# Attention over chunks of 64 tokens and a squared-ReLU feed-forward: token groups formed inside batches, queries loaded token by token, and later slots for the attention steps

## Chip, cores and metric

The kernel runs on one core of a Trainium2 chip. The metric is the device time of the core in microseconds; smaller is better. Times are medians over several executions, and a profile is one execution.

## What is computed

Attention inside chunks of 64 tokens, for 8 batches, 8 heads, 576 tokens (nine chunks) a batch and 64 numbers a head; then a feed-forward layer with a squared ReLU over all 4608 tokens. Inputs and output are float32.

```python
q_c, k_c, v_c = (x.reshape(B, H, S // 64, 64, D) for x in (q, k, v))
scores = np.matmul(q_c, k_c.transpose(0, 1, 2, 4, 3)) / np.sqrt(D)
attn = softmax(scores)
x = np.matmul(attn, v_c)            # back to (B * S, H * D) = (4608, 512)
h = np.maximum(x @ w_in, 0.0)       # w_in 512 x 2048
out = h * h @ w_out                 # w_out 2048 x 512
```

## The kernel before

**Groups and blocks.** The 4608 tokens are cut into 18 groups of 256 (`GT`), in the order of the flat token number. As a batch has 576 tokens, many groups reach over a batch's end; `segments` cuts their loads there, so such a group has more and smaller loads. Two groups make a block of the feed-forward (`blocks`, line 41); there are nine blocks, and the second one takes its groups as [3, 2].

**Loads** all go through the SP queue, in program order. `qk_pieces(g)` loads q and k of a group, `v_pieces(g)` its values, the even heads into `ve_sb` tiles and the odd heads into `vo_sb` tiles; these lie 64 tokens askew, so that a matmul on half of the array finds its chunk in the right half of the partitions. In the types of the load: q comes as pairs of tokens (512 contiguous bytes), k of groups 0 to 3 too, k of the others and v token by token (256 bytes). Ten q and k buffers (five each), five `ve_sb` and eleven `vo_sb` buffers take turns.

**Attention of a group** in steps, named by letters in the schedule: C (`cast_qk`, line 213) makes bfloat16 of q and k, on GpSimd (POOL) for groups under 8, else on ScalarE (ACT); TD (`transpose_qk_dma`, line 223) transposes both with one DMA from the SP queue into `qkT`; SC (`scores`, line 231) does 32 small matmuls on TensorE (PE) and one exponential on ACT; AV (`values`, line 259) does 32 matmuls, and VectorE (DVE) divides by the sums into `x`; XT (`transpose_x`, line 287) transposes x, for groups from 6 on by a DMA from the SP queue. Groups 0 to 3 are transposed on PE instead (TA, TE, TQ, TK). In `scores`, the function `queries` picks the right side of the matmul: for groups from 4 on, the tokens of a pair lie apart in `qkT`, and it reads them with a stride.

**Feed-forward of a block.** `ffn_in` is 16 slots, in each of which PE does four matmuls of 512 columns (line 336), ACT the ReLU (347), DVE or ACT the square (351, 349). Block 1 does it in two halves of 256 columns, so 32 slots. `ffn_out` is 14 slots: a form of the product with seven half products instead of eight (line 404), whose sums DVE makes; results are stored from POOL's queue (`store`, line 420). Block 0 does a plain product (485).

**The order is written out by hand.** [...]In the loop at line 546, the block j gives each slot of its feed-forward at most one load of a later block (`go_slots`) and, by `plan`, the attention steps of the next block's groups (`nxt`: SC, AV, XT) and of the one after it (`far`: C, TD). From block 2 on, `loads` are those of `far`. So SP's queue holds, for each block: loads, two XT, two TD, and the rest; whatever stands behind a transpose waits for that transpose's input.

Of the kernel before, what the change touches and what calls it, by code (L numbers as in the profile page):

```python
# [11 lines left out]
BF16 = mybir.dt.bfloat16  # L12
# [5 lines left out]
def kernel(  # L18
# [22 lines left out]
    blocks = [[0, 1], [3, 2]] + [[g, g + 1] for g in range(4, n_grp, 2)]  # L41
# [34 lines left out]
    def segments(g0, n):  # L76
        while n:
            b, s = divmod(g0, S)
            m = min(n, S - s)
            yield b, s, m  # L80
            g0 += m
            n -= m

    qk = {}

    def runs(g):

        for t in range(GT // 128):
            p = 0
            for b, s, m in segments(g * GT + t * 128, 128):  # L90
                yield t, p, m, b, s
                p += m

    def qk_pieces(g):
# [3 lines left out]

        pairs = ((q_sb, q), (k_sb, k)) if g < FIRST_DMA_T else ((q_sb, q),)
        p = 0  # L100
        for b, s, m in segments(g * GT, GT):
            for dst, src in pairs:
                yield lambda dst=dst, src=src, b=b, s=s, p=p, m=m: nc.sync.dma_start(
                    out=dst.rearrange("p t h d -> p (t h d)")[p:p + m // 2, :].rearrange(
                        "p (h e) -> p h e", h=H),
                    in_=src[b, :, s:s + m, :].rearrange("h (s i) d -> s h (i d)", i=2))
            p += m // 2
        if g < FIRST_DMA_T:
            return
        for t, p, m, b, s in runs(g):  # L110
            yield lambda b=b, s=s, t=t, p=p, m=m: nc.sync.dma_start(
                out=k_sb[p:p + m, t, :, :],
                in_=k[b, :, s:s + m, :].rearrange("h s d -> s h d"))

    def v_pieces(g):

# [4 lines left out]
        for n in {0: [0, 1, 2], 2: [5], 3: [6, 7, 8]}.get(g, [2 * g + 1, 2 * g + 2]):  # L121
            lo, hi = max(0, 128 * n - 64), min(n_tokens, 128 * n + 64)
            p = lo - (128 * n - 64)
            for b, s, m in segments(lo, hi - lo):
                yield lambda n=n, p=p, m=m, b=b, s=s: nc.sync.dma_start(
                    out=v_odd[n % NO][p:p + m, :, 0:D],
                    in_=v[b, 1::2, s:s + m, :].rearrange("h s d -> s h d"))
                p += m
# [102 lines left out]
    def scores(g):  # L231
        qkT = state.pop(("qkT", g))

        def queries(a, t, hp, p):
            x = qkT[64 * a:64 * a + 64, 0]
            if g < FIRST_DMA_T:
                return x[:, t, hp, p * 64:p * 64 + 64]
# [397 lines left out]
```

## Time and profile before

| | us |
|---|---|
| median of 5 executions | 295.82 (290.96 to 297.7) |
| the profiled execution | 294.84 |
| its span, first to last instruction | 293.1 |
| PE busy in it | 275.6 |
| DVE busy | 190.7 |
| ACT busy | 161.9 |
| POOL busy | 53.5 |

The span is what the lines of a profile add up to; the time of an execution has 1.7 us more around it. Busy time is summed over an engine; a busy engine isn't necessarily the one that sets the end. In the answers of the trace, a line such as "153.96 0.69 PE L249 ..." reads: start in us, duration in us, engine, line of the kernel, what it writes and reads, and in brackets how long the engine had been idle and what ended that. SPq is SP's queue: its duration is the time to issue a DMA, the data arrives later.

The DMA queues in the page: 138,640 packets and 47.33 MB on SP's queue (q1), 2,832 packets and 9.18 MB on POOL's (q0). Typical times from issue to landing by its last part: k 256 KB 6.4 us, q 512 KB 6.8, v 128 KB 4.0, the transpose into qkT 5.6, that into xT 3.6.

### The profile page before, as it was taken

Reading aid. Unit: us, or ns where it says so; the run is one execution under the profiler, and the core shown is the slowest. Engines: PE = TensorE matmul, PEld = TensorE weight load, DVE = VectorE, ACT = ScalarE, POOL = GpSimd, SP = SyncE. Lnnn points to the kernel's source line nnn. Section 1 sums busy time; section 2 is a strip of 40 time slices with the busy share of each in tenths; the row PEclk is TensorE's granted clock in tenths of the full one; section 3 lists DMA queues with packets and bytes.
Section 4 is the critical chain, followed back from the end, with each engine's and each line's share of the span. In section 5 each row is a group of like instructions: output and inputs, shape, how many; then the busy total and the mean of one; then the engine's idle time right before and its main releaser. Section 6 shows DMA issues by size and latency. Waiting matters only on the chain.

```text
span 293.1 us, 7263 instructions
## 1 busy us (share of the span) xinstructions
PE 275.6 (94%) x3011; PEld 183.2 (63%) x3014; DVE 190.7 (65%) x305; ACT 161.9 (55%) x270; POOL 53.5 (18%) x85
## 2 busy tenths in 40 slices
PE   2999999999999999999959999999999999999994
PEld 1774444778774488448824686468547854784583
DVE  1157514899863495489634994698369738964793
ACT  1527605776348753866366656773777387317710
POOL 2037644042152003000200002001100210020012
PEclk9999999999999999999999999999999999999999
DMA  7999999997999999999999999998996841111003
GB/s 201 236 303 363 363 314 200 291 216 175 226 227 247 232 198 244 216 231 187 209 231 227 183 154 270 211 153 193 297 215 123 125 166 36 38 77 68 2 18 125
DMA packets 141648, 57.09 MB, mean 195 GB/s; under 512 B 110448, under 2 KB 137328, under 8 KB 141616
## 3 DMA queue, kind: packets, MB, share of 16 engines
q1 hardware_dynamic: 138640, 47.33, 75.6%
q0 software_dynamic: 2832, 9.18, 8.9%
q8 instruction: 23, 0.38, 0.6%
q10 hardware_dynamic: 144, 0.13, 0.1%
q14 instruction: 9, 0.07, 0.1%
HBM read 36.70 MB, written 9.44 MB: 157 GB/s over the span
## 4 chain that ended last, share of the span: by engine, by line
PE 82%; DMA 8%; DVE 5%; ACT 2%; issue 1%; SPq 0%; ACTq 0%
PE ps_ffn L336 36%; PE ps_ffn L404 32%; DMA qkT<-qkb 6%; PE ps_ffn L485 4%; PE ps_att L249 3%; PE ps_att L273 2%; DVE gT L351 2%; DMA k_sb<-in_k_dram 2%; PE ps_ffn L211 2%; DVE x L281 2%; ACT rl L347 1%; PE ps_ffn L165 1%; PE ps_att L300 1%; PE ps_ffn L200 0%; DVE w_out_bf L364 0%
## 5 line engine op out<-in xcount | busy, mean ns | idle before, releaser
L336 PE MATMUL ps_ffn<-xT,w_in_bf 128*128 128x512 bf16 (+1 forms) x640 | 130.5, 358 | 0.8 <-ACT rl L347 0.2
L351 DVE TENSOR_TENSOR gT<-rl 128x512 bf16<-128x512 f32 (+2 forms) x132 | 77.0, 607 | 65.1 <-ACT rl L347 63.5
L347 ACT ACTIVATE rl<-ps_ffn 128x512 f32<-128x512 f32 (+2 forms) x160 | 85.6, 553 | 34.7 <-PE ps_ffn L336 32.7
L336 PEld LDWEIGHTS <-w_in_bf 128*128 128x128 bf16 x640 | 60.6, 98 | 58.9 <-issue 1.5
L404 PEld LDWEIGHTS <-w_st 128*128 128x128 bf16 x640 | 62.3, 98 | 7.5
L423 POOL DMA_DIRECT2D out_dram<-o_sb x29 | 20.8, 717 | 159.4 <-DVE o_sb L364 153.9
L364 DVE TENSOR_TENSOR w_st<-gT 128x2048 bf16<-128x2048 bf16 x40 | 47.3, 1218 | 0.2
L404 PE MATMUL ps_ffn<-w_out_bf,w_st 128*128 128x256 bf16 x384 | 45.0, 273 | 0.0
L404 PE MATMUL ps_ffn<-w_sum,w_st 128*128 128x256 bf16 x256 | 29.6, 273 | 0.0
L404 PEld LDWEIGHTS <-gT 128*128 128x128 bf16 x256 | 25.0, 98 | 4.5
L281 DVE TENSOR_TENSOR x<-ps_att,rec 128x512 bf16<-128x512 f32 x36 | 24.9, 691 | 1.2
L475 ACT COPY o_sb<-ps_ffn 128x512 f32<-128x512 f32 (+1 forms) x8 | 4.5, 560 | 34.7 <-PE ps_ffn L404 34.7
L256 ACT ACTIVATE e<-ps_att 128x1024 bf16<-128x1024 f32 x18 | 17.9, 1020 | 10.0 <-PE ps_att L249 9.7
L349 ACT ACTIVATE gT<-rl 128x512 bf16<-128x512 f32 (+2 forms) x28 | 16.8, 599 | 0.9
L249 PE MATMUL ps_att<-qkT 64*64 64x64 bf16 x576 | 11.4, 219 | 4.3 <-DMA qkT<-qkb 4.0
L404 PE MATMUL ps_ffn<-w_out_bf,gT 128*128 128x256 bf16 x128 | 15.3, 273 | 0.0
L404 PE MATMUL ps_ffn<-w_sum,gT 128*128 128x256 bf16 x128 | 15.3, 272 | 0.0
L485 PE MATMUL ps_ffn<-w_out_bf,gT 128*128 128x512 bf16 x61 | 14.3, 379 | 0.6 <-ACT rl L347 0.3
L249 PEld LDWEIGHTS <-qkT 64*64 64x64 bf16 x576 | 8.8, 109 | 9.2 <-DMA qkT<-qkb 4.3
L273 PEld LDWEIGHTS <-e 64*64 64x64 bf16 x576 | 7.0, 107 | 9.1 <-DVE x L281 2.2
L140 POOL CAST w_in_bf<-w_st 128x1024 bf16<-128x1024 f32 (+1 forms) x9 | 8.6, 966 | 19.8 <-DMA w_st<-in_moe_w_in_dram 19.8
L273 PE MATMUL ps_att<-ve_sb,e 64*64 64x65 bf16 x288 | 9.9, 197 | 1.6 <-DVE x L281 0.7
(51 smaller groups left out, 164.7 us busy)
## 6 DMA issues: line engine op xcount, KB each, us to landing
out_dram<-o_sb POOLq DMA_DIRECT2D x33, 256.0 KB, 5.2
k_sb<-in_k_dram SPq DMA_DIRECT2D x25, 256.0 KB, 6.4
q_sb<-in_q_dram SPq DMA_DIRECT2D x12, 512.0 KB, 6.8
ve_sb<-in_v_dram SPq DMA_DIRECT2D x32, 128.0 KB, 4.0
vo_sb<-in_v_dram SPq DMA_DIRECT2D x32, 128.0 KB, 4.0
w_st<-in_moe_w_in_dram SPq DMA_DIRECT2D x8, 512.0 KB, 7.0
w_st<-in_moe_w_out_dram SPq DMA_DIRECT2D x8, 512.0 KB, 6.9
k_sb<-in_k_dram SPq DMA_DIRECT2D x3, 512.0 KB, 7.1
```

The source lines that it names most:

```text
L249: nc.tensor.matmul(out=ps[64 * c:64 * c + 64, o0:o0 + 64], lhsT=qkT[64 * a:64 * a + 64, 1, t, hp, cols], rhs=queries(a, t, hp, p), start=T ...
L256: nc.scalar.activation(out=e.rearrange("p a h t q -> p (a h t q)"), in_=ps, func=AF.Exp, scale=scale)
L273: nc.tensor.matmul(out=ps[64 * p:64 * p + 64, a, hp * (D + 1):(hp + 1) * (D + 1)], lhsT=e[64 * c:64 * c + 64, a, hp, t, :], rhs=vb[64 * c: ...
L281: nc.vector.tensor_tensor(out=x[:, t].rearrange("p h a d -> p a h d"), in0=o[:, :, :, 0:D], in1=rec.to_broadcast([128, 2, n_hp, D]), op=AL ...
L336: nc.tensor.matmul(out=h[:, 0:n], lhsT=w_in_bf[:, dt, ft * 128:(ft + 1) * 128], rhs=xT[:, c // 128:(c + n) // 128, dt, :], start=(dt == 0) ...
L347: nc.scalar.activation(out=rl[:, 0:n], in_=h[:, 0:n], func=AF.Relu)
L349: nc.scalar.activation(out=gT[:, ft, c:c + n], in_=rl[:, 0:n], func=AF.Square)
L351: nc.vector.tensor_tensor(out=gT[:, ft, c:c + n], in0=rl[:, 0:n], in1=rl[:, 0:n], op=ALU.mult)
L364: engine.tensor_tensor(out=out, in0=in0, in1=in1, op=op)
L404: nc.tensor.matmul(out=outs[t], lhsT=a[:, i, t * 128:(t + 1) * 128], rhs=b[:, i, :], start=(first and i == 0 and (last or t == 0)), stop=( ...
L423: dma.dma_start(out=out[t0:t0 + HT, col:col + HD].rearrange("(t p) d -> p t d", p=128), in_=o_sb.rearrange("p (t d) -> p t d", d=HD))
L485: nc.tensor.matmul(out=o_ps[tt], lhsT=gT[:, ft, tt * 128:(tt + 1) * 128], rhs=w_out_bf[:, ft, :], start=(ft == 0), stop=(ft == n_ft - 1))
```

## The change

1. Groups are formed inside batches: two groups of four whole chunks a batch, and the ninth chunk of each batch goes, four batches together, into two groups of their own, placed as groups 14 and 15 (block 7). Blocks are then simply pairs in order. `runs` gives the pieces of a group; a whole group has no cut.
2. q of groups from 4 on is loaded token by token in two loads, as k is; the cast and the scores read it in order (`queries` is gone). Groups 0 to 3 keep pairs.
3. The odd heads' tiles are laid out for two groups together: five tiles a pair of groups with loads of 64, 128, 128, 128 and 64 tokens (four loads of 128 before, cut at batch ends).
4. A ninth-chunk group is stored with two DMAs in place of one.
5. Slots: in block 1, one slot later for XT of the block's second group, and one earlier for SC, AV and XT of the next block's; in the others, SC, AV and XT mostly one slot later, with three slots between the two groups' AV.

```diff
-    blocks = [[0, 1], [3, 2]] + [[g, g + 1] for g in range(4, n_grp, 2)]
+    blocks = [[g, g + 1] for g in range(0, n_grp, 2)]
+    CH = GT // 4
+    n_ch = S // CH
+    whole = [[(b, CH * (4 * i + c)) for c in range(4)] for b in range(B) for i in range(2)]
+    rest = [[(b, CH * (n_ch - 1)) for b in range(b0, b0 + 4)] for b0 in range(0, B, 4)]
+    chunks = whole[:-2] + rest + whole[-2:]
+    def is_whole(g):
+        return chunks[g][0][0] == chunks[g][3][0]
...
     def runs(g):
-        for t in range(GT // 128):
-            p = 0
-            for b, s, m in segments(g * GT + t * 128, 128):
-                yield t, p, m, b, s
-                p += m
+        for t in range(2):
+            (b, s), (b1, s1) = chunks[g][2 * t:2 * t + 2]
+            if b == b1:
+                yield t, 0, 2 * CH, b, s
+            else:
+                yield t, 0, CH, b, s
+                yield t, CH, CH, b1, s1
...
         for t, p, m, b, s in runs(g):
-            yield lambda b=b, s=s, t=t, p=p, m=m: nc.sync.dma_start(
-                out=k_sb[p:p + m, t, :, :],
-                in_=k[b, :, s:s + m, :].rearrange("h s d -> s h d"))
+            for dst, src in ((q_sb, q), (k_sb, k)):
+                yield lambda dst=dst, src=src, b=b, s=s, t=t, p=p, m=m: nc.sync.dma_start(
+                    out=dst[p:p + m, t, :, :],
+                    in_=src[b, :, s:s + m, :].rearrange("h s d -> s h d"))
...
+    odd_tile, odd_loads = {}, {}
+    n_odd = 0
+    for g in range(n_grp):
+        if is_whole(g):
+            if g % 2 == 0:
+                first = n_odd
+                n_odd += 5
+            b, s = chunks[g][0]
+            for c in range(4):
+                odd_tile[g, c] = first + g % 2 * 2 + (c + 1) // 2
+            odd_loads[g] = [(first, CH, CH, b, s), (first + 1, 0, 2 * CH, b, s + CH),
+                            (first + 2, 0, 2 * CH, b, s + 3 * CH)] if g % 2 == 0 else [
+                                (first + 3, 0, 2 * CH, b, s + CH), (first + 4, 0, CH, b, s + 3 * CH)]
...
-        copy(
-            out=qkb[:, 0].rearrange("p (i h d) -> p i h d", i=2, h=H),
-            in_=q_sb.rearrange("p (h i d) -> p i h d", h=H, i=2))
-        copy(out=qkb[:, 1], in_=k_sb)
+        for which in range(2):
+            copy = nc.gpsimd.tensor_copy if g < 8 else nc.scalar.copy
+            copy(out=qkb[:, which], in_=qk[g][which].rearrange("p t h d -> p (t h d)"))
...
-                            rhs=queries(a, t, hp, p),
+                            rhs=qkT[64 * a:64 * a + 64, 0, t, hp, p * 64:p * 64 + 64],
...
-                        vb = vob[t + p] if a else veb[:, t]
+                        vb = vob[2 * t + p] if a else veb[:, t]
...
+            if not is_whole(g):
+                for p in range(2):
+                    dma.dma_start(
+                        out=out.rearrange("(b s) d -> s b d", s=S)[
+                            s0:s0 + CH, b + p:b + 4:2, col:col + HD],
+                        in_=o_sb[p * CH:(p + 1) * CH].rearrange("p (t d) -> p t d", d=HD))
...
-            for slot, f in ((1, TK), (4, SC), (7, AV), (11, XT)):
+            for slot, f in ((1, TK), (4, SC), (7, AV), (12, XT)):
...
-                for slot, f in ((16 + 4 * i, C), (21 + 4 * i, TD), (37 + i, SC), (39 + 2 * i, AV),
-                                (42 + 2 * i, XT)):
+                for slot, f in ((16 + 4 * i, C), (21 + 4 * i, TD), (36 + i, SC), (38 + 2 * i, AV),
+                                (41 + 2 * i, XT)):
...
-            slots = {SC: (4, 4), AV: (7, 10), XT: (11, 13), C: (18, 22), TD: (20, 24)}
+            slots = {SC: (5, 5), AV: (8, 11), XT: (11, 14), C: (18, 22), TD: (20, 24)}
             if j == 3:
-                slots.update({SC: (6, 6), AV: (9, 11), XT: (12, 14)})
+                slots.update({SC: (6, 6), AV: (9, 12), XT: (12, 15)})
             if j == 2:
-                slots = {SC: (8, 11), AV: (12, 14), XT: (15, 17), C: (20, 23), TD: (22, 25)}
+                slots = {SC: (8, 10), AV: (12, 15), XT: (15, 18), C: (20, 23), TD: (22, 25)}
```

## The prediction

> **What bounds the kernel now.** I read four things in this order: the page's busy shares and slices, the chain of waits, the timelines of PE, ACT and SP around the waits that the chain names, and the DMA view of two short stretches in which only one kind of load moves.
>
> ```profile
> span 293.1 us, 7263 instructions
> ...
> PE 275.6 (94%) x3011; PEld 183.2 (63%) x3014; DVE 190.7 (65%) x305; ACT 161.9 (55%) x270; POOL 53.5 (18%) x85
> ...
> PE   2999999999999999999959999999999999999994
> ...
> DMA  7999999997999999999999999998996841111003
> ```
>
> PE is full but for the start, the end and one slice (the 21st, 146 to 154 us). The DMA row is full as well, up to 205 us. So two resources run side by side, and the question is where PE waits for DMA.
>
> ```profile
> 46.32 0.38 PE ps_att L249 x32
> ...
> 75.23 0.62 PE ps_att L249 x32
> ...
> 113.86 9.21 DMA qkT<-qkb
> 123.11 0.69 PE ps_att L249 x32
> ...
> 145.16 8.75 DMA qkT<-qkb
> 153.96 0.69 PE ps_att L249 x32
> ...
> 182.01 1.11 PE ps_att L249 x64
> ```
>
> The chain (start, duration, what) goes over to a DMA transpose of q and k twice, before the scores of groups 9 and 11 (blocks 3 and 4), and never later. The PE timeline gives the second wait:
>
> ```profile
> 153.96 0.69 PE L249 MATMUL ps_att<-qkT 64*64 64x64 bf16 x32 [3.26 <-DMA qkT<-qkb]
> ```
>
> The same row in block 3 starts at 121.7 and ends at 123.8 where an undisturbed pair of scores takes 1.11: 0.9 us lost there, 3.3 here. Why are these transposes late? Group 10's cast on ACT and its transpose on SP:
>
> ```profile
> 136.75 1.04 ACT L221 CAST qkb<-k_sb 128x1024 bf16<-128x1024 f32 x1
> ```
>
> ```profile
> 140.19 1.28 SPq L125 DMA_DIRECT2D vo_sb<-in_v_dram  x2
> 141.58 8.21 SPq L227 DMA_TRANSPOSE qkT<-qkb  x2
> 149.84 0.58 SPq L103 DMA_DIRECT2D q_sb<-in_q_dram  x1
> ...
> 222.48 1.28 SPq L294 DMA_TRANSPOSE xT<-x  x1
> 226.73 6.72 SPq L227 DMA_TRANSPOSE qkT<-qkb  x2
> ```
>
> The cast is done at 137.8 and the transpose is issued at 141.58, when SP has got through the loads ahead of it. From 44 to 150 us SP never idles over 2 us, and where it does (82.5 to 84.4, 87.0 to 87.9) it waits for a cast that waits for a load. So up to block 4 the loads, casts and transposes on the SP queue are one serial chain: whatever makes a load dearer there arrives at 153.96 in full. Later the chain catches up; before the last pair of transposes SP idles 3.0 us (223.8 to 226.7).
>
> The price of a load by packet size, from two stretches with one kind in flight: q and k in 512-byte packets (5 to 8.5 us), v in 256-byte ones (12 to 14.4 us):
>
> ```profile
> DMA packets 2017, 1.02 MB, mean 290 GB/s; under 512 B 32, under 2 KB 2017, under 8 KB 2017
> ```
>
> ```profile
> DMA packets 2094, 0.54 MB, mean 224 GB/s; under 512 B 2093, under 2 KB 2093, under 8 KB 2093
> ```
>
> **The change part by part.**
>
> *q by single tokens, loads.* For the 14 groups from 4 on, q goes from two tokens (512 bytes) to one token (256 bytes) a packet. A group's q is 524,288 bytes: 1.81 us at 290 GB/s, 2.34 at 224, so +0.53 each. Eight groups (4 to 11) lie ahead of group 11's transpose: +4.2 us on the serial chain; all 14, +7.4. Here a rule speaks against the change. The Trainium skill, "DMA: Bandwidth & Descriptors", section "Why small descriptors are slow (HBM only)", gives a fixed overhead of about 3 cycles beside one cycle per 32 bytes, so 2 x 11 cycles where one 512-byte packet takes 19: +16%, or 1.81 x 0.16 = 0.29 a group and 2.3 on the chain. The same page's "Specifications" puts line rate at 512 bytes and up. The trace has the same two packet sizes 29% apart, so I take the trace: with the rule the forecast below would be 1.9 us lower.
>
> *q by single tokens, scores.* The query operand was read with a stride (token pairs interleaved); now it is contiguous, as it already is for groups 0 to 3. A group's 32 matmuls take 0.38 at 46.32 and 0.62 at 75.23; a pair in one slot 1.11 at 182.01 against 0.76 for two contiguous ones. That is 4 x 0.24 + 5 x 0.35 = 2.7 us of PE. What falls before 153.96 is only a longer wait for the transpose there. After it count 0.24 of block 4's own second group and 3 x 0.35: -1.3.
>
> *q's cast* reads in order instead of by pairs: ACT took 1049 ns for q by pairs and 1046 for k in order, so nothing. POOL casts (groups 4 to 7) cost 1044 and 1375, k the dearer one, and wait for their loads, which hide it.
>
> *Groups inside batches.* The built programs give the loads on SP's queue: ahead of group 11's transpose 109 before and 110 after, group 13's 125 and 127, group 15's 142 and 152, group 17's 156 and 176. So the split loads at batch borders that go are replaced by q in two loads and five odd-head v loads a pair of groups; bytes are equal. One more load on the chain to group 11 is at most 0.6 us of SP (its rows are 0.45 to 0.65 when not held up), at least nothing: I take 0, as DMA and not SP holds it for q and k. In block 2 about 256 KB of v that went ahead of the transposes now goes behind them: that lightens block 3's wait by 1.2 and burdens block 4's equally, no effect at 153.96.
>
> *Block order [2, 3]* swaps two groups; the same bytes before block 0's last slots, nothing.
>
> *Stores of the ninth-chunk groups:* eight of 128 KB for four of 256 KB on POOL, 4 x 0.72 us on an engine that waits 153.9 us for DVE at this line; hidden. Without that cover it would be 2.9 us.
>
> *Slots.* Scores move from slot 4 to 5 from block 4 on: PE does one more slot (12 matmuls in 2.70 at 154.65, so 4 in 0.9) ahead of the wait: -0.9 at 153.96. x comes one slot later with its values, and so does its second transpose. Behind one on SP stand the rest of the loads and both qkT transposes, so a wait for x would hold them up; in block 5 DVE ended x at 189.15 and SP came to it at 190.67, and a slot later makes 190.1, so the wait stays away by 0.6 us (without that cover, up to 0.9 a block on SP's chain). In block 1 the scores, values and transposes of groups 4 and 5 come one slot earlier (36 for 37), which takes up to 0.4 us off the stall before block 2, but asks for group 4's transpose at about 74 where it landed at 74.3 and now lands 1.1 later: a wait of up to 1.5. Both ends lie ahead of 153.96 and cancel against the wait there. The same holds for the wider spacing of the values in blocks 2 and 3, where the second group's values take 0.8 to 1.1 us against 0.4 undisturbed: up to 1.9, but into the wait.
>
> *Sum:* 293.1 + 4.2 - 0.9 - 1.3 = 295.1. The profiled execution took 294.84, 1.74 over its span, so 296.8, +0.7%. It lies 0.3% under the median of 295.82; the same ratio on the median gives 297.8, and I say 298. Bounds of the unknowns: the load price 2.3 to 6 (the transposes, 3.7 to 9.2 us to landing, can stretch with it), the new waits in block 1 nothing to 1.5, so 294 to 301.5 for this case.
>
> **The rivals.**
>
> *The chain of loads is not what ends last, and PE is.* For it: two executions of before took 291, so with luckier DMA most of the 4.2 us of waits go. Then the change is worth its PE part: 2.7 of scores, 0.4 and 0.5 at the two x transposes of block 1, 1.9 of values, and the 4.2 of waits: 9.7 off, 283.4 of span, 286 on the median's scale. Against it: the SP queue without a pause from 44 to 150 us, and dearer loads.
>
> *The ninth-chunk block chokes SP (slower).* In block 5 the loads for groups 14 and 15 go from 17 ahead of the last transpose to 25, and 24 instead of 14 follow up to group 17's. At 0.6 us of SP each that is +4.8 and +6.0, with q's 0.5 a group on top. Cover: group 15's transpose (issued 201.74, 5.6 to landing) is 3.2 us ahead of its scores at 210.5, the later slot adds 0.9, SP's idle time before group 16's adds 3.0, group 17's landing (230.2 + 6.8) is 1.9 ahead of 239.0. That leaves about 1.9 late in block 6 and 5.5 in block 7: 7.4 more, 302.5 of span, 305 on the median's scale, +3%. It decides from some 0.3 us of SP per extra load. Against it: half-sized loads are issued faster where the queue was held up by bytes.
>
> *The change doesn't do what it says:* the scores gain nothing, if the stride is not why they took 0.62. Then +1.3: 299.
>
> **How the numbers follow.** Forecast 0.45 (with the no-gain case), all within 2% of before, 2% being about what a measurement of this kernel tells from no change; PE-bound rival 0.20, faster than 290 for nearly all of it; SP-choked rival 0.35, over 301.7. Faster 0.19, same 0.46, slower 0.35. The range is 287 to 306: it holds the forecast and most of both rivals; likeliest case alone 294 to 302.
>
> **What would show it.** Scores at 0.38 a group after group 3; q loads in 256-byte packets and some 14,300 more packets on q1 (138,640 now); PE's wait for the transpose in block 4 at 5 to 7 us where it was 3.3; block 5 starting about 3 us later than 177.7; blocks 5 to 7 at 28.1 us each against 28.5. A period over 29 in blocks 6 or 7 with a wait for qkT is the slower rival; no wait at all in blocks 3 and 4 is the faster one, and proves the serial chain wrong.

## The result, and the profile after

| | us |
|---|---|
| before, 71 executions beside the changed kernel | 292.47 (289.92 to 299.29) |
| changed kernel, 36 executions | 293.37 (289.43 to 297.6) |
| ratio of the two | 1.0034, interval 1.0014 to 1.0054 |
| profiled execution of the changed kernel | 289.43, span 287.6 |

The change costs 0.3% where 0.7% was forecast; both lie within the 2% that the forecast counted as no change. Most of the distance between the 298 forecast and the 293.4 measured is the base: 295.82 was the median of five executions, 292.47 is that of 71. Two things must be kept apart in what follows: the profile of before shown above was an execution with long waits (294.84), that of the changed kernel is the shortest of its 36. Their spans differ by 5.5 us; that is not what the change is worth. The ratios of two kernels, here and below, are formed from the executions within 1.5% of each kernel's fastest; where the medians of all executions say something else, they stand beside. Two more measurements of the changed kernel, told below, gave 1.0121 and 0.9998 (the second with its stores called later in the program, which moved nothing). So from one measurement to the next a ratio moves by more than its own interval says, and no term below is surer than about 0.6%, or 2 us.

The page of the changed kernel, the rows that were shown of before:

```profile
span 287.6 us, 7298 instructions
...
PE 270.7 (94%) x3011; PEld 179.3 (62%) x3014; DVE 189.0 (66%) x305; ACT 161.7 (56%) x270; POOL 57.0 (20%) x89
...
PE   2999999999999999999879999999999999999994
...
DMA  7999999999999999999999999579898951132003
...
q1 hardware_dynamic: 153296, 47.33, 77.5%
```

PE is as full as before and has one thin place, slices 20 and 21, again around 145 us. SP's queue moves the same bytes in 14,656 more packets. The PE timeline there (start, duration, and in brackets the idle time and what ended it):

```profile
142.36 5.35 PE L344 MATMUL ps_ffn<-xT,w_in_bf 128*128 128x512 bf16 x24 [0.96 <-DMA xT<-x]
148.21 0.45 PE L257 MATMUL ps_att<-qkT 64*64 64x64 bf16 x32 [0.50 <-DMA qkT<-qkb]
149.70 0.45 PE L257 MATMUL ps_att<-qkT 64*64 64x64 bf16 x32 [1.04 <-DMA qkT<-qkb]
```

There are three waits in block 4 now, 2.5 us together, where there was one of 3.26 and where the forecast looked for one of 5 to 7: for the transpose of x at the block's start, which no step of the forecast held, and for q and k of groups 10 and 11. SP's queue ahead of them:

```profile
137.26 1.25 SPq L302 DMA_TRANSPOSE xT<-x  x1
138.60 1.45 SPq L145 DMA_DIRECT2D vo_sb<-in_v_dram  x1
140.15 7.52 SPq L243 DMA_TRANSPOSE qkT<-qkb  x2
```

Groups 10 and 11's transposes are issued from 140.15, where the profile before had 141.58. PE asks for them at 147.7 and 148.7; before, it asked for group 11's at 150.7. So PE comes 2 us earlier and the transposes 1.4, and they still meet here. Against a second profile of before (below), in which they were issued at 140.42, the transposes are hardly earlier at all.

Later blocks, in windows of one block each (length, then busy time by engine); first before, then the changed kernel:

```profile
177.66:206.16 28.50, 28.45 (x306) 18.74 (x304) 20.69 (x31) 18.28 (x28) 2.87 (x5) 1.00 0.99 200
206.16:234.66 28.50, 28.45 (x306) 18.73 (x304) 20.68 (x31) 18.27 (x28) 2.88 (x5) 1.00 0.88 191
```

```profile
171.94:200.47 28.53, 28.01 (x307) 18.35 (x304) 20.54 (x31) 18.30 (x28) 2.86 (x5) 1.00 0.85 180
200.47:228.99 28.52, 28.01 (x307) 18.36 (x305) 20.44 (x31) 18.27 (x28) 2.86 (x5) 1.00 1.03 204
```

PE's busy time (the first number after the length) fell by 0.44 a block, as the contiguous scores promised (0.71 for a pair of groups at 177.22, 1.11 before), and the block takes as long as before. The gain became idle time. What PE's two queues waited for ahead of the value matmuls of block 5 says where:

```profile
  DVE rec L280: 0.4, 1
  ACT rl L347: 0.4, 1
  DVE x L281: 0.2, 1
```

```profile
  DVE x L289: 1.6, 3
  ACT rl L355: 0.4, 1
```

First before, then the changed kernel (idle summed over the matmul and the weight queue). In the changed kernel both halves of the second group's values wait for DVE to finish an x.

### The profile page after: what moved, and what is told of

Its sections match the earlier page's. It is cut to its first block, busy times and chain, and to the rows that moved or that the text cites. A ratio compares the mean times of both kernels' runs of the same rounds, so it can differ in the third digit from the quotient of the medians.

```text
span 287.6 us, 7298 instructions
## 1 busy us (share of the span) xinstructions
PE 270.7 (94%) x3011; PEld 179.3 (62%) x3014; DVE 189.0 (66%) x305; ACT 161.7 (56%) x270; POOL 57.0 (20%) x89
## 4 chain that ended last, share of the span: by engine, by line
PE 58%; DMA 14%; SPq 10%; DVE 5%; ACT 4%; issue 4%; POOL 3%; ACTq 0%; POOLq 0%
PE ps_ffn L412 31%; PE ps_ffn L344 25%; DMA w_st<-in_moe_w_in_dram 5%; DMA qkT<-qkb 3%; SPq L145 3%; DVE gT L359 3%; ACT rl L355 2%; DMA q_sb<-in_q_dram 2%; SPq L141 2%; SPq L106 2%; DMA w_st<-in_moe_w_out_dram 2%; POOL qkb L237 2%; DVE x L289 2%; DMA xT<-x 2%; ACT e L264 2%
## 5 line engine op out<-in xcount | busy, mean ns | idle before, releaser
L359 DVE TENSOR_TENSOR gT<-rl 128x512 bf16<-128x512 f32 (+2 forms) x132 | 75.4, 606 | 64.0 <-ACT rl L355 62.9
L440 POOL DMA_DIRECT2D out_dram<-o_sb x25 | 17.8, 714 | 129.1 <-DVE o_sb L372 124.5
L237 POOL CAST qkb<-q_sb 128x1024 bf16<-128x1024 f32 x4 | 6.9, 1726 | 23.0 <-DMA q_sb<-in_q_dram 21.1
L237 ACT CAST qkb<-k_sb 128x1024 bf16<-128x1024 f32 x10 | 10.5, 1047 | 1.6 <-DMA k_sb<-in_k_dram 1.6
```

The costliest lines, as they stand in the source:

```text
L237: copy(out=qkb[:, which], in_=qk[g][which].rearrange("p t h d -> p (t h d)"))
L359: nc.vector.tensor_tensor(out=gT[:, ft, c:c + n], in0=rl[:, 0:n], in1=rl[:, 0:n], op=ALU.mult)
L440: dma.dma_start(out=out[t0:t0 + HT, col:col + HD].rearrange("(t p) d -> p t d", p=128), in_=o_sb.rearrange("p (t d) -> p t d", d=HD))
```

## The experiments

Stage lengths below are taken from the PE timeline, from the first matmul of a layer to the first of the next; "in 4" is the first layer of block 4 with the attention steps in it, "out 4" the second. T4 is when SP issues the transpose of group 4, the first one of the serial chain: it shows how early the loads are.

| us | before, again | slots alone | groups alone | groups + slots, q in 512 B | changed kernel |
|---|---|---|---|---|---|
| in 1 | 17.88 | 16.70 | 16.95 | 16.40 | 16.47 |
| in 2 | 17.27 | 16.24 | 17.26 | 16.25 | 15.78 |
| out 2 | 12.23 | 14.50 | 12.23 | 12.38 | 12.36 |
| in 3 | 17.21 | 16.36 | 17.20 | 16.34 | 16.34 |
| out 3 | 12.23 | 15.18 | 12.23 | 12.23 | 13.35 |
| in 4 | 16.96 | 18.07 | 17.30 | 16.38 | 17.36 |
| in 5 | 16.26 | 16.38 | 16.26 | 16.37 | 16.30 |
| T4 | 69.61 | 69.06 | 65.75 | 66.43 | 68.94 |

**Before, once more, unchanged.**

> The kernel before, unchanged, for a second profile. Theory A (loads, casts and transposes on SP's queue are one serial chain that sets the scores of group 11): the PE waits for qkT in blocks 3 and 4 show again, 2 us or more together, and qkT of group 11 lands at 152 to 155 us. Theory B (the chain has slack, the first profile met an unlucky execution): the waits are under 1 us together and the span is about 289 us. In both: blocks 5 to 7 take 28.5 us each.

291.7 us in its one execution, span 289.9. On the PE timeline one wait for the transposes is left in block 4:

```profile
150.81 0.69 PE L249 MATMUL ps_att<-qkT 64*64 64x64 bf16 x32 [0.52 <-DMA qkT<-qkb]
```

So most of the wait of 3.26 belonged to the first profile's execution: here the chain of loads ends within about half a microsecond of when PE asks for it. With the two that close, dearer loads and a faster PE can both bring the wait back.

**q in 256-byte packets, alone.**

```diff
+            if g >= FIRST_DMA_T:
+                for i in range(2):
+                    yield lambda b=b, s=s, p=p, m=m, i=i: nc.sync.dma_start(
+                        out=q_sb.rearrange("p t h d -> p (t h d)")[p:p + m // 2, :].rearrange(
+                            "p (h i d) -> p h i d", h=H, i=2)[:, :, i, :],
+                        in_=q[b, :, s:s + m, :].rearrange("h (s i) d -> s h i d", i=2)[:, :, i, :])
```

> The kernel before, with q of groups from 4 on loaded in two loads of 256-byte packets into the same places (pair layout): the price of the smaller packets alone, scores still read with a stride. Theory A: +0.53 us a group on the chain, qkT of group 11 about 4 us later than in before, the whole 3 to 4.5 us slower (ratio 1.010 to 1.015). Theory B: the loads hide behind PE, under 1 us (ratio under 1.004).

Ratio 1.0197, interval 1.0151 to 1.0244: 5.8 us. The medians of all executions are only 2.2 us apart (296.78 of 6, 294.59 of 43 of before): before's run from 289.43 to 299.56, this kernel's from 295.41 to 298.59, so the short executions are missing and the long ones are no longer than before. One q load becomes two here, so this is the price of smaller packets and more loads together.

In the two profiles the first layer of block 4 takes 21.50 for 16.96, and the other layers are the same. The PE timeline, then windows before and after 153.3 (the last three numbers are granted clock, DMA share, GB/s):

```profile
151.08 0.69 PE L257 MATMUL ps_att<-qkT 64*64 64x64 bf16 x32 [1.82 <-DMA qkT<-qkb]
152.62 0.71 PE L257 MATMUL ps_att<-qkT 64*64 64x64 bf16 x32 [0.85 <-DMA qkT<-qkb]
153.26 5.29 PE L344 MATMUL ps_ffn<-xT,w_in_bf 128*128 128x512 bf16 x12
```

```profile
149.30:153.30 4.00, 1.37 (x65) 1.12 (x66) 1.29 (x2) 1.62 (x3) 0.00 (x0) 0.79 1.06 276
153.30:158.60 5.30, 5.30 (x28) 1.68 (x28) 0.69 (x1) 2.86 (x5) 0.00 (x0) 0.52 1.30 216
```

Two waits of 2.7 us together, against 0.5 in the run above, are only half of these 4.5 us: group 11's scores start at 152.62 where they started at 150.81. After them 12 matmuls take 5.29 us where they take 2.70 at full clock: the granted clock was 0.52. A wait is paid twice when it brings the clock down.

**Contiguous scores, alone** (before, with queries in two runs of 32, the exponential writing them back in order).

```diff
-            return x[:, :, hp, p0:p0 + 32].rearrange("c i p -> c p i")
+            return x[:, :, hp, p0:p0 + 32]
...
+                out=e.rearrange("p a h t (r i) -> p (a h t) i r", i=2),
+                in_=ps.rearrange("p (x i r) -> p x i r", i=2, r=32), func=AF.Exp, scale=scale)
```

> The kernel before, with the queries of a chunk read as two contiguous runs of 32 (even tokens, then odd ones) instead of pair by pair, and the exponential writing them back in order: scores without the stride, loads as before. Theory A: a group's scores fall from 0.62 to 0.4 us, but what is gained ahead of group 11 is waited for; 1.1 us faster (0.996). Theory B: PE sets the end throughout, 2.5 to 3 us faster (0.990 to 0.992).

Ratio 1.006, interval 1.0035 to 1.0085, but the medians of all executions point the other way (292.75 against 294.59), so in time neither gain nor loss can be told. A pair of scores takes 0.71 instead of 1.11, but the exponential that writes with gaps takes 1306 ns instead of 1024, and the weight loads of the values wait for it and then for DVE:

```profile
182.04 0.34 PEld L278 LDWEIGHTS <-e 64*64 64x64 bf16 x32 [0.42 <-ACT e L260]
...
185.47 0.21 PEld L278 LDWEIGHTS <-e 64*64 64x64 bf16 x16 [0.77 <-DVE x L286]
186.32 0.21 PEld L278 LDWEIGHTS <-e 64*64 64x64 bf16 x16 [0.63 <-DVE x L286]
```

The gain on PE is real, and the first layers of blocks 5 to 7 take 16.60 all the same, 16.26 before: what comes after the scores is ACT and DVE, and they became no faster.

**The changed kernel with the old slots from block 4 on.**

```diff
-            slots = {SC: (5, 5), AV: (8, 11), XT: (11, 14), C: (18, 22), TD: (20, 24)}
+            slots = {SC: (4, 4), AV: (7, 10), XT: (11, 13), C: (18, 22), TD: (20, 24)}
```

> The changed kernel, with SC, AV and XT back at slots 4, 7 and 10, 11 and 13 from block 4 on. Theory A (the later slot gives the late transposes 0.9 us): the wait for qkT in block 4 grows by 0.9, and it is as fast as the changed kernel or up to 1 us slower. Theory B (the later scores push both exponentials onto the square of ft 14 that ACT does in slot 6, DVE falls behind, and the second values wait 0.5 us in each of blocks 5 to 7): the second group's values go back from 1.10 to about 0.6 us, blocks 5 to 7 from 28.5 to 28.0 each, 1.0 to 1.9 us faster than the changed kernel, 0.996 of before or less.

Ratio 1.0012, interval 0.9973 to 1.005; blocks 5 to 7's first layers 16.12 for 16.30, so 28.35 us a block for 28.53, where theory B had 28.0. No difference from the changed kernel in time can be told: the slot of the scores in these blocks is not what decides.

**Groups and slots, q back in 512-byte packets.** One load of q for a whole group, read with a stride:

```diff
+        if is_whole(g):
+            b, s = chunks[g][0]
+            yield lambda b=b, s=s: nc.sync.dma_start(
+                out=q_sb.rearrange("p t h d -> p (t h d)").rearrange("p (h e) -> p h e", h=H),
+                in_=q[b, :, s:s + GT, :].rearrange("h (s i) d -> s h (i d)", i=2))
...
```

> The changed kernel, with q of whole groups from 4 on loaded as before: token pairs in 512-byte packets, one load a group, scores with the stride. So groups and slots alone. Theory A (the 256-byte packets of q are what keeps the loads late in block 4): PE's waits for xT and qkT in blocks 3 and 4 fall from 3 to under 1 us, the first layer of block 4 takes 16.3 to 16.8 us; blocks 5 to 7 as in the changed kernel; 2 us faster than the changed kernel (0.995 of before). Theory C (groups and slots bring PE to block 4 earlier than the loads come, whatever their packets): waits of 2 us or more in block 4 stay, as fast as the changed kernel within 1 us.

Ratio 0.9885, interval 0.985 to 0.9921. In its profile PE waits for no transpose, and its row in the page has no thin place:

```profile
PE   2999999999999999999999999999999999999994
```

```profile
69.61 3.79 SPq L227 DMA_TRANSPOSE qkT<-qkb  x2
```

```profile
66.43 5.34 SPq L253 DMA_TRANSPOSE qkT<-qkb  x2
```

These are group 4's transposes in before, again, and in this run. Other profiles differ less: with these groups and q in 512-byte packets, seven profiles (the holds further down left out) have it at 65.8 to 68.5, and four with before's groups and packets at 68.1 to 70.4, so it is 2.3 us earlier on average. Group 10's comes at 136.2 to 139.7 against 139.8 to 142.4, 3.0 us earlier. SP's rows say what stands ahead of groups 10 and 11's transposes: 109 loads in before, 102 here, 110 in the changed kernel, where each of eight groups has a second q load. So the whole groups alone save seven loads; whether their number, their cuts or the odd heads' new layout is why the chain is earlier was not separated.

Against the changed kernel (1.0034) this is 1.5%, or 4.4 us, for q's packets with their second loads, less what the contiguous scores may be worth, as this run reads them with the stride. What is left of the change, groups and slots, gains 1.15%, or 3.4 us.

**The same with contiguous scores** (queries in two runs, the exponential reading its input out of order and writing in order).

```diff
...
+                out=e.rearrange("p a h t (r i) -> p (a h t) r i", i=2),
+                in_=ps.rearrange("p (x i r) -> p x r i", i=2, r=32), func=AF.Exp, scale=scale)
```

> The same, but the queries are read as two contiguous runs of 32 and the exponential reads its input in the tokens' order from PSUM. Scores without the stride and loads in 512-byte packets. If reading PSUM with a stride costs ACT nothing (1.02 us an exponential), scores take 0.64 a pair and the time is 0.5 to 1 us under that with the stride; if the exponential takes 1.3 us as with the strided write, the values wait longer and it is 0.5 to 1 us over it.

Ratio 0.9924, interval 0.9894 to 0.9955; the exponential stays at 1017 ns. So reading out of order is free here where writing with gaps was not. A gain of the contiguous scores cannot be told, as above. This run and the changed kernel both read the scores without the stride; from this pair q's packets and second loads are worth 1.1%, 3.2 us, and groups with slots 0.8%, 2.2 us.

**Where the scores' gain went.** ACT squares tile 14 in slot 6, next to the two exponentials. Moved to tile 5 (slot 13):

```diff
-            if (n == 512 and ft in SQUARES_ON_ACT) or (n < 512 and ft in (12, 3)):
+            if (n == 512 and ft in (SQUARES_ON_ACT if j < 4 else (10, 3, 5))) or (n < 512 and ft in (12, 3)):
```

> The changed kernel, with ACT's square moved from slot 6 (ft 14) to slot 13 (ft 5) in blocks from 4 on. Theory B (exponentials and that square pile up on ACT, DVE falls behind, the second group's values wait): the second group's values go from 1.10 to about 0.5 us and the first layer of blocks 5 to 7 from 16.29 to 15.8 us each, 1.5 us in all. If ACT's pile is not the cause, they stay at 1.10 and 16.29.

First layers of blocks 5 and 6: 15.75 for 16.30. The two ACT timelines, changed kernel first:

```profile
177.88 1.94 ACT L264 ACTIVATE e<-ps_att 128x1024 bf16<-128x1024 f32 x2
179.69 0.62 ACT L355 ACTIVATE rl<-ps_ffn 128x512 f32<-128x512 f32 x1
180.34 0.63 ACT L357 ACTIVATE gT<-rl 128x512 bf16<-128x512 f32 x1
180.87 1.81 ACT L355 ACTIVATE rl<-ps_ffn 128x512 f32<-128x512 f32 x3
```

```profile
183.21 1.93 ACT L264 ACTIVATE e<-ps_att 128x1024 bf16<-128x1024 f32 x2
185.02 1.60 ACT L355 ACTIVATE rl<-ps_ffn 128x512 f32<-128x512 f32 x3
187.36 0.60 ACT L355 ACTIVATE rl<-ps_ffn 128x512 f32<-128x512 f32 x1 [0.74 <-PE ps_ffn L344]
```

In the first, after 1.94 us of exponentials the square holds back the ReLUs, DVE gets its squares late, and x after them; in the second ACT has caught up and idles 0.74 by the fifth ReLU. This is a place at which 0.5 us a block was lost. The square was not moved in the kernel before, nor with strided scores, so how much of the 0.55 is the scores' own gain is open. In time the gain is not shown: the ratio is 0.9917, interval 0.9876 to 0.9959, but from 4 of its 23 executions, and the medians of all are 292.08 and, of before, 291.59. The profiled execution took 299.15, with a wait for x and, in block 7, one for q and k, which comes up again under the rivals:

```profile
146.59 8.06 PE L344 MATMUL ps_ffn<-xT,w_in_bf 128*128 128x512 bf16 x24 [4.80 <-DMA xT<-x]
...
242.54 0.64 PE L257 MATMUL ps_att<-qkT 64*64 64x64 bf16 x32 [3.60 <-DMA qkT<-qkb]
```

**Slots alone** (before's groups and loads, the new slots).

> The kernel before with the slots of the changed one: the slots alone. The changed kernel gained 1.4 us in the first layer of block 1, 1.5 in block 2 and 0.9 in block 3. If the slots are why: the same here less the stride (0.24 a group of scores), so 1.4, 1.0 and 0.5. If the groups are why, the first layers stay at 17.8, 17.3 and 17.2 us. Block 4 then waits for the same loads as before; blocks 5 to 7 get slower, 16.7 us against 16.26. On the whole within 1 us of before.

Ratio 1.0025, interval 0.9991 to 1.0058. The slots do what the table shows in the first layers of blocks 1 to 3 (1.2 + 1.0 + 0.9 us less), and in the profile, of an execution 3.5 us over this kernel's median, the second layers of blocks 2 and 3 give more than that back, in waits for x:

```profile
116.06 6.22 PE L336 MATMUL ps_ffn<-xT,w_in_bf 128*128 128x512 bf16 x28 [1.95 <-DMA xT<-x]
147.59 7.04 PE L336 MATMUL ps_ffn<-xT,w_in_bf 128*128 128x512 bf16 x24 [2.79 <-DMA xT<-x]
```

PE is earlier, the loads are not (T4), and x's transpose stands behind them on SP.

**Groups alone** (q in 512-byte packets, the old slots).

> The groups alone: groups inside batches, q of whole groups loaded once in 512-byte packets and read with a stride, and all slots as they were before the change. Theory A (the groups make the chain of loads earlier, and this is a gain by itself where PE waited for the chain): group 4's transpose is issued at about 66.5 as in the kernel with groups and slots (69.6 before), no wait for qkT over 0.3 us in blocks 3 and 4; blocks 1 to 3 of the first layer as before (17.8, 17.2, 17.2), block 4 about 16.5, blocks 5 to 7 16.26; span 288.5 to 289.5, ratio to before 0.985 to 0.998. Theory B (the groups are worth something only together with the slots): span 290 to 291, ratio 0.998 to 1.004. Theory C (the slots give all, the groups nothing, and the run with the slots alone was disturbed by something else): group 4's transpose at 69 to 69.6 and qkT waits of 1 us or more in block 4.

Ratio 0.9989, interval 0.99 to 1.0078. T4 is 3.9 us earlier than in before, again, as theory A had it, but the ratio shows no gain, and the profile met a late transpose in block 6 (first layer 21.52):

```profile
209.03 0.64 PE L267 MATMUL ps_att<-qkT 64*64 64x64 bf16 x32 [2.98 <-DMA qkT<-qkb]
```

Groups alone make the loads early, slots alone make PE early, and each by itself finds the other as it was; both together gained 1.15%, or 0.8% when the scores are contiguous. For the slots alone the missing gain is shown. For the groups alone it is not: the interval allows up to 1%, and the medians of all executions (292.79 of 6, 294.79 of 11) are 0.7% apart. Its shortest executions speak for no gain: 290.91, 290.86 in before beside it, where groups with slots reached 287.6.

**All that gained, together:** groups, slots, q in 512-byte packets read through the exponential, and the moved square.

> The groups and the slots of the change, q of whole groups loaded once in 512-byte packets and reordered by the exponential's read, and ACT's square of tile 14 moved to tile 5 from block 4 on. Theory A (the second group's values wait for DVE, which waits for ACT's square between the two exponentials): blocks 5 to 7 of the first layer 15.75 instead of 16.30, second values at 0.4; as the loads are early, no wait for xT or qkT over 0.5 us; span 283 to 284, ratio to before 0.975 to 0.985. Theory B (PE that is faster by 0.55 a block runs into the transposes again, as it did in the run with q token by token): a wait for xT or qkT of 0.5 to 3 us in blocks 5 to 7 and a ratio of 0.985 to 0.993, no better than without the moved square.

> The kernel with the groups and slots of the change and q of whole groups loaded once in 512-byte packets, reordered by the exponential's read, once more, beside the same with the moved square, on one chip. Up to block 4 the two programs are the same. Theory A (the gain of groups and slots holds on any chip): ratio to before 0.985 to 0.995, blocks 5 to 7 16.3, lowest times 287 to 288. Theory B (whether the transposes of x and of q and k land in time is chance, and the first measurement was a lucky one): ratio 0.995 to 1.002, and a wait for xT or qkT of 1 us or more in blocks 3 or 4.

> The same with ACT's square of tile 14 moved to tile 5 from block 4 on, once more. Theory A (0.55 us a block, 2.2 us in all, come on top): blocks 5 to 7 15.75, lowest times 285 to 286, ratio 0.975 to 0.988. Theory B (PE that is faster from block 5 on waits for transposes instead): lowest times 286 to 288, ratio within 0.004 of the kernel without the moved square, and waits for qkT or xT in blocks 6 and 7 of 0.5 to 1.5 us.

The first time 0.9971, interval 0.9896 to 1.0047 (medians of all executions 291.79 and 294.79); then, side by side on another chip, 0.9926 (0.9892 to 0.996) without the moved square and 0.9863 (0.9786 to 0.9939) with it. The first layers of blocks 5 and 6 are 15.75 each time, as theory A says; and PE, faster, meets waits for x of 2.3 to 2.6 us at the start of block 4 with and without the square, as theory B says. Neither is refuted. This version is faster than both kernels, than before by about 1.4% in two of its three measurements (see the run below with the stores moved in the program only); what the moved square alone adds in time is not separated, as the intervals overlap.

**The wait for x at the start of block 4.** It is the new wait of this change. It looked as if the stores of block 3, which a faster PE brings forward, slowed the second transpose of x: it lands in 3.4 to 3.7 us when the first store follows 2 to 3.3 us later, in 5.0 to 7.3 when they go side by side. The changed kernel again, and with the stores of block 3 called later in the program:

```diff
+            if j in (3,) and not now:
+                later.append(lambda: store(dma, o_sb, half, col, t, True))
+                return
...
+                if slot == 8:
+                    while later:
+                        later.pop(0)()
...
```

> The changed kernel itself once more, as the partner of the next run on the same chip. Theory A (a second x transpose that meets the first store of the block's product lands late): its second x transpose of block 4 is issued after about 136.5, the first store of block 3 at 137 to 138, landing takes 4.5 us or more and PE waits 1 to 3 us at the start of block 4. Theory B (chance): issue and landing have no bond; landing 3.4 to 3.7 as often as not.

> The changed kernel with the four stores of block 3's product held back to slot 8 of block 4. Theory A (block 3's stores, which come 4 us earlier now, take the DMA engines from the x and q/k transposes): second x transpose of block 4 lands in 3.4 to 3.8 us, no wait for xT at the start of block 4, and groups 10 and 11's transposes land 1 us or more sooner, so that the waits there fall from 1.0 + 1.5 to under 1; median 1 to 2.5 us lower than the changed kernel's on the same chip. Theory B (the transposes are late because they are issued late, behind the loads on SP; the stores have no part): landing 4.5 us or more as in the changed kernel, same waits, medians within 0.7 us.

> The version with groups, slots, q in 512-byte packets and the moved square, with the stores of blocks 2 and 3 held back to slot 8 of the next block. Theory A: no wait for xT in blocks 3 and 4 (2.3 to 2.6 us before), ratio to before 0.97 to 0.982, lowest times 284 to 285.5. Theory B: the same waits, ratio 0.983 to 0.992.

1.0121 (1.0062 to 1.0181), 0.9998 (0.9959 to 1.0037), and 0.9862 (0.9823 to 0.9902) for the best version. The last two moved nothing: POOL has no other work at that place, so it issues a store as soon as DVE is done, at 140.49 in the profile. They answer no question about stores; they are repeats, of the changed kernel and of the best version. The first shows the wait at its longest, and its second cost in the two windows ahead of it and behind it:

```profile
148.96 8.02 PE L344 MATMUL ps_ffn<-xT,w_in_bf 128*128 128x512 bf16 x24 [4.80 <-DMA xT<-x]
```

```profile
136.90:142.25 5.35, 5.35 (x52) 4.79 (x50) 5.23 (x7) 2.56 (x3) 0.71 (x1) 1.00 1.16 226
148.96:156.98 8.02, 8.02 (x32) 3.00 (x36) 2.23 (x4) 3.50 (x6) 0.00 (x0) 0.66 1.19 260
```

The 24 matmuls that took 5.35 us in the profile above took 8.02 at a clock of 0.66. Then the stores were really held back, behind a small copy on POOL that waits for group 11's transpose:

```diff
...
+                if slot == 8 and later:
+                    nc.gpsimd.tensor_copy(out=mark, in_=state["last"][:, 0, 0, 0, 0:1])
...
```

> The changed kernel with the four stores of block 3's product held back behind a one-column copy on GpSimd that waits for group 11's transpose (moving them alone in the program, as two runs ahead of this one did, left their times as they were, since GpSimd has nothing else to do there). Theory A (block 3's stores, which come 4 us earlier now, slow the second x transpose and groups 10 and 11's transposes): the stores are issued at about 150 instead of 137 to 145; the second x transpose of block 4 lands in 3.4 to 3.8 us where the changed kernel had 4.5 to 6.9; PE waits under 0.5 us for xT there, if SP issues it by 139; the transposes of groups 10 and 11 land in 5 to 7 us instead of 7 to 10; ratio to before 0.990 to 0.998. Theory B (the transposes are late because SP's queue is late, or because the two kinds of transposes hinder each other): second x transpose still 4.5 us or more, PE waits 1 to 3 us at the start of block 4, ratio 1.000 to 1.008.

> The version with groups, slots, q in 512-byte packets and the moved square, with the stores of blocks 2 and 3 held back in the same way, behind the transposes of groups 9 and 11. Theory A: second x transposes of blocks 3 and 4 in 3.4 to 3.8 us, no wait for xT (1.9 to 2.6 us without the holding back), ratio 0.970 to 0.982. Theory B: same waits, ratio 0.983 to 0.992.

> The changed kernel with block 3's four stores held back until group 11's transpose has landed, as in the held run ahead of this one, but with the small tile of the wait made 64 bytes wide: at 2 bytes (32 reserved) it had moved every later tile by 32 bytes, so that none began at a multiple of 64 any more, and loads were late from block 1 on, ahead of the stores held back. Theory C (that shift made the held run slower): blocks 1 to 3 as in the changed kernel (out of block 1 15.5 to 16.3, block 2's product under 16.5, not 19.0 and 19.8), median under 296. Theory A on the stores (they slow the transposes): second x transpose of block 4 in 3.4 to 4 us, PE waits under 0.5 us for xT, groups 10 and 11's transposes land in 4.4 to 5.5 us; ratio to before 0.988 to 0.998. Theory B (lateness of SP's queue): second x transpose 4.5 us or more or issued after 140, PE waits 1 to 3 us at the start of block 4, ratio 1.000 to 1.010. Theory D (the hold itself costs, by stores that meet block 4's loads): blocks 6 or 7 with a wait for qkT of over 1 us.

Ratios 1.0258 (1.0187 to 1.0329), 1.0057 (1.0013 to 1.0102) and 1.0225 (1.0162 to 1.0288): all worse than without the hold (for the second, the best version, the medians of all executions are 293.56 and 295.0, where it had 288.88 and 293.44 without). In the last, SP and POOL:

```profile
145.78 1.24 SPq L303 DMA_TRANSPOSE xT<-x  x1
...
147.83 5.51 SPq L243 DMA_TRANSPOSE qkT<-qkb  x2
```

```profile
156.31 2.83 POOL L444 DMA_DIRECT2D out_dram<-o_sb  x4 [0.29 <-DVE gT L360]
```

With no store near, the transposes of groups 10 and 11 landed in 5.0 and 4.4 us, and in 4.4 to 5.2 in the two other held profiles; in those of the changed kernel without the hold it was anything from 3.9 to 10.0. That speaks for theory A as to them. The second transpose of x still took 4.8 and PE waited 2.35: for x the stores are not the cause, or not the only one. It is issued at 145.78, where the profile with q in 512-byte packets has 135.23, because SP comes to it late. And the hold made the whole slower for a reason that is not settled: in both held profiles of the changed kernel block 1's second layer takes 19.0 to 19.3 us (15.9 without), 60 us ahead of the stores that were held. Behind them, theory D's sign is there too: the last run's profile waits 2.71, 3.36 and 1.63 us for q and k in blocks 5, 6 and 7. Theory C, that the small tile shifted the others, fell with the last run.

## Why the forecast was off by half

- **q's small packets, +4.2: the right size, not quite for the right reason.** Measured 5.8 us alone on before (2.2 by the medians of all executions), 3.2 and 4.4 on the changed kernel from two pairs. But in the two profiles on before only 1.8 us of it is the chain coming later (group 11's scores at 152.62 for 150.81; the first profile of before, with 153.96, was later than both), less than the 2.3 of the forecast's rule, and the rest is the clock after the wait, which no step held. On the changed kernel the chain does move by more: group 10's transposes are issued at 140.2 to 145.5 in five profiles, at 136.2 to 139.7 with q in 512-byte packets. That the price came so near 4.2 is in part luck, and these runs do not decide between the trace's 29% and the rule's 16%.
- **"Groups inside batches ... I take 0, as DMA and not SP holds it": this is the step that failed.** The count of 109 loads before and 110 after was right, but eight of the 110 are q's second loads, which belong to the other part of the change. The groups without them have 102, seven fewer, and SP comes to group 4's transpose 2.3 us earlier and to group 10's 3.0, on average, on the very chain that was priced.
- **"Both ends lie ahead of 153.96 and cancel against the wait there", for the slots of blocks 1 to 3: true only if the loads stay where they are.** With slots alone it held (3.1 us gained in first layers, taken by waits, ratio 1.0025). With the loads earlier the slots' gain came through in the two profiles without the moved square taken first: the first layers of blocks 1 to 3 keep it and no second layer waits. In four later ones 1.9 to 2.6 us of it went into the wait for x at block 4 again. Two edits costed at nothing, each with its own reason, were worth 3.4 us together in one run, 2.2 in another; how much of this the groups would bring alone is open, as said.
- **Contiguous scores after block 4, -1.3: measured 0.** PE's busy time fell as forecast, the length of blocks 5 to 7 did not: the values wait for DVE, and DVE for ACT. The forecast named what hides the gain before 153.96 but did not ask the same question behind it.
- **Score slot, -0.9:** not told apart from nothing (1.0012 against 1.0034).
- **The rivals.** In its own profile the changed kernel has no wait for q and k in blocks 6 and 7, but the rival of the ninth-chunk groups was not empty: of the 15 profiles of kernels with these groups eight, three of them with held stores, wait there for the transposes of groups 14 to 17, by 0.9 to 4.6 us, and of the five with before's groups none does. These transposes have more loads ahead of them than before (group 17's 176 on SP in the changed kernel, 164 with q in one load, 156 in before). That this is why was not tried. PE did not become the bound. The wait for the transpose was named for q and k only; the longest of the new ones is for x, whose transpose stands in the same queue behind the same loads.

In sum: +4.4 for the packets, -3.4 for groups with slots, 0 for the scores, +1.0 in all (0.34% of 292.5), where the forecast had +4.2 - 0.9 - 1.3 = +2.0. The first two come from one run between the two kernels, so they must add up to the result; the other run gives +3.2 and -2.2. The forecast came as near as it did by luck: the 2.2 us that it claimed for scores and slot, and that did not come, stood in for most of what it left out at groups and slots.

What is open: why the second x transpose takes 3.4 to 3.7 us in some executions and 4.8 to 7.3 in others, what makes the transposes of groups 14 to 17 late in half of the profiles, and why holding the stores made earlier blocks slower.

## What to carry to other kernels

When two chains run neck and neck, here loads and PE, an edit that makes one of them earlier may be worth nothing by itself, as the slots here, and something together with an edit that helps the other: cost them together, against each other, not each against the old wait. Count the loads of each part of a change separately; here one part's saving hid behind another part's cost. After every gain on an engine ask who is next on the way to the next wait; here ACT's order beside two exponentials held 0.55 us a block. Before moving a DMA in the program, see whether its queue holds anything else: on an idle queue the place in the program decides nothing.

## What the hardware showed that was not expected

- A wait of PE can cost about its own length again, and its length does not say whether it will. After 1.8 + 0.9 us of waits the clock was 0.52 for 5 us; after one of 4.8 it was 0.66 over 8 us; after one of 2.98 (groups alone) 0.50. Yet the 3.26 us wait in the first profile of before left it at 1.00, as did one of 3.36 (stores held, the last run), and of two waits of 2.30 us for x at the start of block 4, one in each of the first two runs of the best version, the first left it at 1.00 and the second brought it to 0.76 over 7 us. The waits of over 3.5 us for a transpose (five in these profiles, 3.58 to 4.80) all brought it down. The Trainium skill, "TensorE: Matmul & The Clock Gate", Part 1, has the clock fall after an idle window of some 3.4 us, in a window that runs freely. That fits the chance in it, by where in the window a wait happens to lie; but waits shorter than a whole such window brought it down here, so the measurement decides, and no run tried the reason.
- The exponential took 1306 ns when it wrote with a stride of two elements and 1017 when it read with a stride of 32 and wrote in order, as against 1024 for both in order.
- Queries with a stride of one token pair cost a pair of scores 1.11 us, contiguous ones 0.71, at the same number of matmuls.
- The transpose of one group's q and k, the same bytes each time, took from 3.6 us (before, again) to 11.2 us (the best version with stores held) to land.
